# Two transformer layers for one token: attention summed in PSUM quadrants and added to the transposed x, x's rows kept as one PSUM sum, the last softmax ahead of the product before it, 22 arena units kept between the layers

## The chip, the core and the metric

One core of a Trainium2 chip runs the whole program. It has TensorE (matmuls, with a weight load before each), VectorE, ScalarE and GpSimd, SyncE whose queue issues the large transfers here, and 16 DMA engines that bring data from HBM into the on-chip memory (SBUF). Matmuls write to PSUM. The metric is the device time of one execution in microseconds; the time before is 1360.39 us, the median of three runs (1358.34 to 1362.09).

## What is computed

Two batch rows, one new token each, width D = 448. An attention block over a cache of 4096 keys and values (16 heads of 256), then a gated feed-forward block, then both once more with the same weights and the same cache.

```python
def _A_ref(x, k_cache, v_cache, wq, wo):
    q = (x @ wq).reshape(B, Sq, H, Dh).transpose(0, 2, 1, 3)
    scores = jnp.einsum("bhqd,bhkd->bhqk", q, k_cache) * (Dh ** -0.5)
    p = _softmax(scores, axis=-1)
    o = jnp.einsum("bhqk,bhkd->bhqd", p, v_cache)
    return o.transpose(0, 2, 1, 3).reshape(B, Sq, H * Dh) @ wo
def _B_ref(x, W_gate, W_up, W_down):
    gate, up = x @ W_gate, x @ W_up
    return (gate * (gate > 0) * up) @ W_down
x = A_x
x = x + _A_ref(_layernorm(x), A_k_cache, A_v_cache, A_wq, A_wo)
x = x + _B_ref(_layernorm(x), B_W_gate, B_W_up, B_W_down)
x = x + _A_ref(_layernorm(x), A_k_cache, A_v_cache, A_wq, A_wo)
x = x + _B_ref(_layernorm(x), B_W_gate, B_W_up, B_W_down)
```

All data is float32. A pass over the cache is 32 units (head and batch row), each with 4 MiB of keys (k) and 4 MiB of values (v): 256 MiB a pass, twice.

## The kernel before

**Storage.** An arena in SBUF holds 27 slots of 1 MiB: six blocks of four slots and three single slots. A k or v of a unit fills a block or four slots, one quarter each. A head's projection weights (`w_head`: wq and wo of one head) go into a single slot; a `w_in` piece (seven of them, gate and up weights) or `w_out` piece (four, down weights) into any. `pending` is the list of transfers in their order; `pump` issues the next one as soon as a slot is given back by `release`, and SyncE's queue runs them in that order. Which slot a transfer gets is settled when the program is built; on the chip it waits for the last reader of that slot. Eight semaphores take turns, so a transfer also waits until the one issued eight before it has landed. `grouped` decides which k and v are one transfer of 4 MiB and which are four of 1 MiB: the first `SMALL` and the last `ENDS` keys of a pass are cut into quarters.

**Kept units.** The second pass runs over the units in reverse order. What the first pass uses last (the head weights of head 15 and `KEPT` = 20 quarters: k of its last three units and v of its last two) stays in the arena and isn't loaded again. That leaves 6 slots for the feed-forward weights between the passes.

**Order of work.** `attention` is a loop over u with a software pipeline written out by hand. In round u: VectorE scores unit u (32 multiply-and-sum instructions, eight for each quarter, `score`); TensorE, VectorE and ScalarE do the softmax of unit u - 1 in pieces (`softmax_turn`, `softmax_exp`, `softmax_sum`) between the quarters; TensorE multiplies the weights of unit u - 1 with its v (`weigh`, 16 matmuls that trace as 32 records, four column groups of PSUM at a time); ScalarE copies that out (`out_copy`); and unit u - 2 is turned (`out_turn`, `out_keep`) and, for every second unit, projected with wo into `acc` (`project`). Each engine runs its instructions in the order written. Scores of kept units are written to PSUM scratch (`pf`) rather than over the k.

**Between the passes.** `acc` is a PSUM sum that starts with x itself (`seed`). `ffn` takes it, subtracts the mean (`center`: statistics, aggregate and subtraction on VectorE, a turn on TensorE, copies), so that `xr` holds the centred x transposed, 16 times side by side; multiplies with the gate pieces, then with the up pieces (`proj`, four column groups), squares and sums for the deviation, forms the product, turns it, and multiplies with w_out. After the first feed-forward the result is not centred anew: its row sums and its turned rows are added to `xr` (lines 495 to 519), and x's rows are put together again a little later for the next `acc` (`rows`, `keep_rows`, two copies to `x_sb`).

## Time and profile before

| | |
|---|---|
| median of three runs | 1360.39 us |
| the profiled execution | 1357.76 us, span 1355.9 us |
| TensorE, VectorE, ScalarE busy | 54%, 57%, 9% of the span |
| chain that ended last | VectorE 43%, unknown queue 26%, DMA 25%, TensorE 4% |
| HBM read | 563.61 MB, 416 GB/s over the span |
| mean granted TensorE clock | 0.704 |

The page gives busy time by engine, the span in 40 slices, the transfer queues and the costliest groups. Beside it the trace can be asked for stretches of time (busy time of each engine in turn with its instruction count, the granted clock of TensorE, the share in which the 16 DMA engines were busy, GB/s), for the chain of waits, for one engine's timeline (start, length, engine, line, operation, out<-in, count, idle time before and what ended it), and for the transfers of one line with their time from issue to landing.

### The profile page before, as it was taken

The numbers are of one execution on the slowest core, as the hardware profiler recorded it, in microseconds if no ns is written. First come the engines' busy times: TensorE is split into PE (matmuls) and PEld (weight loads), VectorE is DVE, ScalarE is ACT, GpSimd is POOL, SyncE is SP. The second block draws the span as 40 slices with busy tenths as digits, with TensorE's granted clock in tenths as the row PEclk, the third lists the DMA queues.
The fourth block names the chain that finished last, engine by engine and source line by source line (L and its number), as shares of the span: only waits on it lengthen the run. The fifth ranks groups of instructions, "written<-read, shape, count | busy, mean of one in ns | idle before, by whom it ended". The sixth has DMA issues, their size and how long they took to land.

```text
span 1355.9 us, 13276 instructions
## 1 busy us (share of the span) xinstructions
PE 733.1 (54%) x3908; PEld 333.9 (25%) x3908; DVE 778.8 (57%) x4474; ACT 119.5 (9%) x312; POOL 0.7 (0%) x6
## 2 busy tenths in 40 slices
PE   2545546555445553554576674545356464554647
PEld 2322212222122221222232332222122221222212
DVE  6564564645646556456629884554645546556461
ACT  1100000000000000000111110000000000000001
POOL 0000000000000000000000000000000000000000
PEclk7667667775676776767796777676676666776669
DMA  9999999999999999999969999999999999999994
GB/s 402 435 432 428 429 432 429 434 429 427 431 429 430 433 430 427 431 428 434 366 255 404 430 429 431 428 429 431 430 429 432 431 430 429 430 427 434 432 409 184
DMA packets 27585, 564.48 MB, mean 416 GB/s; under 512 B 3060, under 2 KB 3064, under 8 KB 9848
## 3 DMA queue, kind: packets, MB, share of 16 engines
q1 hardware_dynamic: 27508, 563.63, 97.6%
q8 instruction: 31, 0.51, 0.2%
q14 instruction: 42, 0.34, 0.1%
q10 hardware_dynamic: 4, 0.00, 0.0%
HBM read 563.61 MB, written 0.00 MB: 416 GB/s over the span
## 4 chain that ended last, share of the span: by engine, by line
DVE 43%; another core or an unknown queue 26%; DMA 25%; PE 4%; issue 1%; ACT 0%; SPq 0%; DVEq 0%; ACTq 0%
DVE arena L303 38%; DMA arena<-in_k_cache_dram 21%; DVE pf L303 3%; DMA arena<-in_w_in_dram 2%; DMA arena<-in_w_out_dram 2%; PE acc L384 1%; PE po L349 1%; PE pq L250 1%; DVE m L321 1%; DVE ri L339 1%; PE pf L437 0%; DVE mx L312 0%; DVE ri L337 0%; SPq L115 0%
## 5 line engine op out<-in xcount | busy, mean ns | idle before, releaser
L303 DVE SCALAR_TENSOR_TENSOR arena<-arena 128x256 f32<-128x256 f32 x1952 | 686.6, 414 | 489.0 <-DMA arena<-in_k_cache_dram 465.6
L349 PE MATMUL po<-arena,probs 128*2 128x512 f32 x2048 | 304.3, 744 | 58.1 <-DMA arena<-in_v_cache_dram 58.0
L323 PE MATMUL small<-m,ones 1*128 1x1 f32 x128 | 36.3, 351 | 398.2 <-DVE m L321 398.2
L303 DVE DVE_READ_ACCUMULATOR arena<-arena 128x1 f32 x1952 | 149.8, 77 | 0.0
L250 PE MATMUL pq<-arena,xr 128*128 128x256 f32 x384 | 123.1, 467 | 14.4 <-DMA arena<-in_w_head_dram 12.9
L323 PEld LDWEIGHTS small<-m,ones 1*128 1x128 f32 x128 | 30.9, 298 | 403.8 <-DVE m L321 398.0
L349 PEld LDWEIGHTS po<-arena,probs 128*2 128x2 f32 x2048 | 53.8, 97 | 253.2 <-issue 188.5
L384 PE MATMUL acc<-arena,oT 128*2 128x448 f32 x128 | 97.1, 910 | 25.4 <-DVE oT L376 25.4
L250 PEld LDWEIGHTS pq<-arena,xr 128*128 128x128 f32 x384 | 85.8, 240 | 70.8 <-DMA arena<-in_w_head_dram 50.6
L367 PE MATMUL small<-ri,row 128*128 128x1 f32 x512 | 67.4, 253 | 33.3 <-ACT row L360 33.3
L367 PEld LDWEIGHTS small<-ri,row 128*128 128x128 f32 x512 | 61.9, 191 | 47.1 <-ACT row L360 47.1
L360 ACT ACTIVATE row<-po 128x512 f32<-128x512 f32 x64 | 38.2, 597 | 383.6 <-PE po L349 383.6
L333 PE MATMUL small<-rs,ones 128*128 128x1 f32 x128 | 37.3, 360 | 59.6 <-ACT probs L329 59.6
L326 ACT ACTIVATE nm<-small,nsr 128x1 f32<-128x1 f32 x64 | 16.7, 262 | 520.8 <-PE small L323 520.8
L333 PEld LDWEIGHTS small<-rs,ones 128*128 128x128 f32 x128 | 31.8, 309 | 65.0 <-ACT probs L329 65.0
L258 PEld LDWEIGHTS pq<-arena,xr 128*128 128x128 f32 x256 | 44.0, 215 | 4.7
L258 PE MATMUL pq<-arena,xr 128*128 128x128 f32 x256 | 43.7, 299 | 0.0
L275 ACT ACTIVATE arena<-pq 128x512 f32<-128x512 f32 x29 | 17.3, 598 | 273.1 <-PE pq L258 273.1
L303 DVE SCALAR_TENSOR_TENSOR pf<-arena,pq 128x256 f32<-128x256 f32 x64 | 26.2, 442 | 12.8 <-ACT row L360 7.4
L384 PEld LDWEIGHTS acc<-arena,oT 128*2 128x2 f32 x128 | 10.8, 103 | 66.4 <-issue 38.3
L329 ACT ACTIVATE probs<-scores,nm,sr 128x32 f32<-128x32 f32 x64 | 26.4, 413 | 2.1
L316 PE MATMUL small<-ident,mx 128*1 128x128 f32 x64 | 17.4, 272 | 15.4 <-DVE mx L312 15.4
(80 smaller groups left out, 185.5 us busy)
## 6 DMA issues: line engine op xcount, KB each, us to landing
arena<-in_k_cache_dram SPq DMA_DIRECT2D x59, 4096.0 KB, 50.9
arena<-in_v_cache_dram SPq DMA_DIRECT2D x59, 4096.0 KB, 54.8
arena<-in_w_head_dram SPq DMA_DIRECT2D x31, 896.0 KB, 42.1
arena<-in_w_in_dram SPq DMA_DIRECT2D x14, 896.0 KB, 22.7
arena<-in_v_cache_dram SPq DMA_DIRECT2D x12, 1024.0 KB, 38.9
arena<-in_k_cache_dram SPq DMA_DIRECT2D x8, 1024.0 KB, 7.1
arena<-in_w_out_dram SPq DMA_DIRECT2D x4, 896.0 KB, 12.6
arena<-in_w_out_dram SPq DMA_DIRECT2D x4, 672.0 KB, 12.8
```

The costliest lines, as they stand in the source:

```text
L250: nc.tensor.matmul(pq[:, b, :], xT[:, c, b : b + 1].to_broadcast([P, P]), w[:, c * DH : (c + 1) * DH], start=(c == 0), stop=False,)
L258: nc.tensor.matmul(pq[:, b, j * P : (j + 1) * P], xT[:, FULL + j, b : b + 1].to_broadcast([P, P]), w[:, FULL * DH : FULL * DH + P], start= ...
L275: nc.scalar.activation(q, pq, AF.Copy)
L303: nc.vector.scalar_tensor_tensor(prod, kt[:, t, :], 1.0, q_of[u], op0=ALU.mult, op1=ALU.mult, accum_out=s_of[u][:, n : n + 1],)
L316: nc.tensor.transpose(p1, mx_of.pop(u), ident)
L323: nc.tensor.matmul(p2, ones[:1].to_broadcast([1, P]), m1, start=True, stop=True)
L329: nc.scalar.activation(p_of[u], s_of.pop(u), AF.Exp, bias=nm, scale=sr[:, b : b + 1], accum_out=rs)
L333: nc.tensor.matmul(r_of[u], ones.to_broadcast([P, P]), rs, start=True, stop=True)
L349: nc.tensor.matmul(po_of[u][32 * t : 32 * t + 2, :], p_of[u][:, n : n + 2], vt[:, 2 * t * DH : (2 * t + 2) * DH], start=(c == 0), stop=(c ...
L360: nc.scalar.activation(row, po_of.pop(u), AF.Copy)
L367: nc.tensor.matmul(pT_of[u][:, c : c + 1], row[:, at : at + P], r_of[u][:, i : i + 1], start=(i == 0), stop=(i == 1),)
L384: nc.tensor.matmul(acc, oT_of[h][:, c, :], wo[:, c * D : (c + 1) * D], start=False, stop=(u == n_u - 1 and c == 1),)
```

## The change

It does six things. `acc` becomes a whole PSUM tile: the projections of successive units go to three row quadrants (rows 0, 32, 64) instead of two rows. A helper `absorb` replaces `center` and the lines that added the feed-forward result: it copies the given rows to SBUF with their row sums, forms minus the mean by a small matmul, turns the rows by matmuls with `lead` (which also sums the quadrants), and adds both to `xr`. x's rows are one PSUM sum `y` (rows 96 and 97 of the same tile) over the whole program, to which `add_rows` adds with one matmul each time; `x_sb`, `seed`, `rows` and `keep_rows` go. In the last round of a pass, the turn and exponential of the last unit come before the v product of the unit before it. `ENDS` goes from 4 to 12, so the last k and the last two v of a pass come in quarters. And one more v quarter is kept (22 units with the head weights), with the first head transfer of the second pass behind three k quarters.

```diff
-SMALL = 14
-ENDS = 4
+SUMS = 96
+SMALL = 13
+ENDS = 12
...
     keep = {of_second[0], *[key for key in of_second if key[0] != "h"][:KEPT]}
+    keep.add(("v", second[2], NC - 1))
     of_second = [key for key in of_second if key not in keep]
+    of_second.insert(NC - 1, of_second.pop(0))
...
-    x_sb = consts.tile([B, D], F32, name="x_sb")
-    nc.scalar.dma_start(x_sb, x.rearrange("b s d -> (b s) d"))
+    nc.scalar.dma_start(row[:B, :D], x.rearrange("b s d -> (b s) d"))
...
-    acc = ps_a.tile([B, D], F32, name="acc")
-    def seed(y):
-        nc.tensor.matmul(y, ident[:B, :B], x_sb, start=True, stop=False)
+    acc = ps_a.tile([P, D], F32, name="acc")
+    nc.vector.memset(acc, 0.0)
+    y = acc[SUMS : SUMS + B]
...
-    def center(y):
-        st = work.tile([B, 6], F32, name="st")
-        nc.vector.bn_stats(st, y)
-        mv = work.tile([B, 2], F32, name="mv")
-        nc.vector.bn_aggr(mv, st)
-        nc.vector.tensor_scalar_sub(row[:B, :D], y, mv[:, 0:1])
+    def absorb(rows, n, rhs, nrhs):
+        sums = work.tile([P, 1], F32, name="sums")
+        nc.scalar.activation(row[:n, :D], rows, AF.Copy, accum_out=sums[:n])
+        minus = ps_s.tile([P, B], F32, name="small")
+        nc.tensor.matmul(minus, sums[:n].to_broadcast([n, P]), nrhs[:n], start=True, stop=True)
         pt = ps_s.tile([P, DC, B], F32, name="small")
-        turned(pt, row[:B], ident[:B, :B], start=True, stop=True)
-        for p, c in spans:
-            x_c = pt[p, c, None, :]
-            nc.vector.tensor_copy(xr[p, c], x_c.to_broadcast([x_c.shape[0], x_c.shape[1], 16, B]))
+        turned(pt, row[:n], rhs[:n], start=True, stop=True)
+        less = work.tile([P, B], F32, name="less")
+        nc.vector.tensor_copy(less, minus)
+        for part in (less[:, None, :].to_broadcast([P, DC, B]), pt):
+            for p, c in spans:
+                x_c = xr[p, c]
+                nc.vector.tensor_add(x_c, x_c, part[p, c, None, :].to_broadcast(x_c.shape))
+    def add_rows(n, rhs, start=False, stop=False):
+        nc.tensor.matmul(y, rhs[:n], row[:n, :D], start=start, stop=stop)
...
             for c in range(2):
+                n = u - 1 + c
+                at = 32 * (n % 3)
                 nc.tensor.matmul(
-                    acc, oT_of[h][:, c, :], wo[:, c * D : (c + 1) * D],
-                    start=False, stop=(u == n_u - 1 and c == 1),
+                    acc[at : at + B], oT_of[h][:, c, :], wo[:, c * D : (c + 1) * D],
+                    start=(n < 3), stop=(n >= n_u - 3),
                 )
...
-            if_pair(softmax_turn, u - 1)
+            if u < n_u:
+                if_pair(softmax_turn, u - 1)
...
-            if_pair(softmax_exp, u - 1)
+            if u < n_u:
+                if_pair(softmax_exp, u - 1)
...
             if_pair(softmax_max, u)
+            if u == n_u - 1:
+                softmax_turn(u)
+                softmax_exp(u)
             for c in range(NC):
                 if_pair(weigh, u - 1, c)
...
-        center(acc)
-        nc.scalar.activation(x_sb, acc, AF.Copy)
+        absorb(acc[:SUMS], SUMS, lead, nlead)
         total = squares()
...
+        add_rows(SUMS, lead)
         deviation(total)
...
         if last:
-            return rows()
...
+            nc.scalar.activation(row[:, :D], pd, AF.Copy)
+            add_rows(P, scaled, stop=True)
+        else:
+            absorb(pd, P, scaled, nscaled)
+        return scaled
...
-    center(x_sb)
+    absorb(row[:B, :D], B, ident[:, :B], nident)
+    add_rows(B, ident[:, :B], start=True)
     attention(first, keep, lambda: None)
-    rows = ffn(False)
-    attention(second, set(), lambda: keep_rows(rows()))
-    nc.vector.tensor_copy(row[:B, :D], ffn(True))
+    scaled = ffn(False)
+    attention(second, set(), lambda: add_rows(P, scaled))
+    ffn(True)
+    found = row[SUMS : SUMS + B, :D]
+    nc.vector.tensor_copy(found, y)
```

On TensorE, where the first pass ends and the first feed-forward begins. Before (`small` is a small PSUM tile, `po` the v products of a unit, `pf` the feed-forward sums):

```order
L349 MATMUL po<-arena,probs 2x512 x16
L316 MATMUL small<-ident,mx 1x128
L367 MATMUL small<-ri_2836,row 128x1 x4
L323 MATMUL small<-m_2864,ones 128x1
L333 MATMUL small<-rs,ones 128x1
L349 MATMUL po<-arena,probs 2x512 x16
L367 MATMUL small<-ri_2879,row 128x1 x4
L384 MATMUL acc<-arena,oT 2x448 x2
L203 MATMUL small<-ident,row 128x2 x3
L205 MATMUL small<-ident,row 64x2 x2
L437 MATMUL pf<-arena,xr 32x448 x16
```

Now:

```order
L329 MATMUL small<-ident,mx 1x128
L336 MATMUL small<-m_2855,ones 128x1
L346 MATMUL small<-rs,ones 128x1
L362 MATMUL po<-arena,probs 2x512 x16
L380 MATMUL small<-ri_2849,row 128x1 x4
L362 MATMUL po<-arena,probs 2x512 x16
L380 MATMUL small<-ri_2892,row 128x1 x4
L399 MATMUL acc<-arena,oT 2x448 x2
L221 MATMUL small<-nlead,sums 128x2
L209 MATMUL small<-lead,row 128x2 x3
L211 MATMUL small<-lead,row 64x2 x2
L455 MATMUL pf<-arena,xr 32x448 x16
```

The three matmuls of the last softmax (`mx`, `m`, `rs`) stand ahead of both v products; the two products have only the turn of the former between them; and the sum of the mean (`nlead`) is a matmul ahead of the turn of x.

On SyncE's queue, from the last k of the first pass to the first transfers of the second. Before:

```order
L115 DMA arena<-in_k_cache_dram 128x8192
L115 DMA arena<-in_v_cache_dram 128x8192
L115 DMA arena<-in_v_cache_dram 128x2048 x4
L115 DMA arena<-in_w_in_dram 128x1792 x7
L115 DMA arena<-in_w_out_dram 128x1792
L115 DMA arena<-in_w_out_dram 128x1344
L115 DMA arena<-in_w_out_dram 128x1792
L115 DMA arena<-in_w_out_dram 128x1344
L115 DMA arena<-in_w_head_dram 128x1792
L115 DMA arena<-in_k_cache_dram 128x2048 x4
L115 DMA arena<-in_v_cache_dram 128x2048 x4
L115 DMA arena<-in_w_head_dram 128x1792
```

Now:

```order
L117 DMA arena<-in_k_cache_dram 128x2048 x4
L117 DMA arena<-in_v_cache_dram 128x2048 x8
L117 DMA arena<-in_w_in_dram 128x1792 x7
L117 DMA arena<-in_w_out_dram 128x1792
L117 DMA arena<-in_w_out_dram 128x1344
L117 DMA arena<-in_w_out_dram 128x1792
L117 DMA arena<-in_w_out_dram 128x1344
L117 DMA arena<-in_k_cache_dram 128x2048 x3
L117 DMA arena<-in_w_head_dram 128x1792
L117 DMA arena<-in_k_cache_dram 128x2048
L117 DMA arena<-in_v_cache_dram 128x2048 x3
L117 DMA arena<-in_w_head_dram 128x1792
```

The last k and both last v of the first pass come in quarters, the head's weights moved behind three k quarters, and the v that follows has three quarters instead of four.

Of the seven w_in pieces, the sixth now waits for the slot of the first w_in piece, the seventh for that of the second; before, the seventh waited for the first. The first k quarter of the second pass takes the slot of the last w_in piece, the next two those of the first two w_out pieces, and the fourth that of the first kept k quarter to be scored; before, the four took the slots of the four w_out pieces, and the first v quarter that of the first kept k quarter.

More of the change, by code (lines that the diff above doesn't have):

```diff
@@ L176, in two_layers @@
     nc.vector.reduce_sum(lead, ident.rearrange("p (m r) -> p r m", r=32)[:, :2], axis=AX.X)
+    nlead = consts.tile([P, B], F32, name="nlead")
+    nc.vector.tensor_scalar_mul(nlead, lead, -1.0 / D)
     sel = consts.tile([P, B], F32, name="sel")
@@ L396, in attention @@
         begun()
-        seed(acc)
         ahead = 2 if ("k", order[0], 0) in keep else 0
@@ L494, in ffn @@
             release("out", "", j)
-        dn = row[:, :D]
-        sums = work.tile([P, 1], F32, name="sums")
-        nc.scalar.activation(dn, pd, AF.Copy, accum_out=sums)
-        def rows():
-            y = ps_f.tile([P, D], F32, name="pf")[:B]
-            seed(y)
-            nc.tensor.matmul(y, scaled, dn, start=False, stop=True)
-            return y
-        if last:
-            return rows()
-        minus = ps_s.tile([P, B], F32, name="small")
-        nc.tensor.matmul(minus, sums.to_broadcast([P, P]), nscaled, start=True, stop=True)
-        pt = ps_s.tile([P, DC, B], F32, name="small")
-        turned(pt, dn, scaled, start=True, stop=True)
-        less = work.tile([P, B], F32, name="less")
-        nc.vector.tensor_copy(less, minus)
-        for part in (less[:, None, :].to_broadcast([P, DC, B]), pt):
-            for p, c in spans:
-                x_c = xr[p, c]
-                nc.vector.tensor_add(x_c, x_c, part[p, c, None, :].to_broadcast(x_c.shape))
-        return rows
-    def keep_rows(rows):
-        nc.scalar.activation(x_sb, rows, AF.Copy)
-    center(x_sb)
-    attention(first, keep, lambda: None)
-    rows = ffn(False)
-    attention(second, set(), lambda: keep_rows(rows()))
-    nc.vector.tensor_copy(row[:B, :D], ffn(True))
-    nc.sync.dma_start(out.rearrange("b s d -> (b s) d"), row[:B, :D])
+        if last:
+            nc.scalar.activation(row[:, :D], pd, AF.Copy)
[3 more added lines that the diff above has]
+        return scaled
+    nident = work.tile([B, B], F32, name="nident")
+    nc.vector.tensor_scalar_mul(nident, ident[:B, :B], -1.0 / D)
+    absorb(row[:B, :D], B, ident[:, :B], nident)
+    add_rows(B, ident[:, :B], start=True)
+    attention(first, keep, lambda: None)
+    scaled = ffn(False)
[3 more added lines that the diff above has]
+    nc.vector.tensor_copy(found, y)
+    nc.sync.dma_start(out.rearrange("b s d -> (b s) d"), found)
 _OUTS = [((B, 1, D), "float32")]
```

## The prediction

> **What bounds the kernel now.** I read the page first, then the stretches of time around the two feed-forward parts, then the chain of waits, then single transfers and the engines' timelines there.
>
> ```profile
> span 1355.9 us, 13276 instructions
> DMA  9999999999999999999969999999999999999994
> q1 hardware_dynamic: 27508, 563.63, 97.6%
> q8 instruction: 31, 0.51, 0.2%
> 300.00:600.00 300.00, 152.74 (x808) 69.47 (x807) 171.12 (x1000) 23.85 (x64) 0.00 (x0) 0.69 1.00 430
> ```
>
> The transfer queue is busy 97.6% of the span and no compute engine is near that. In the steady stretch it moves 430 GB/s, so a quarter of a k or v block (1,048,576 bytes) costs 2.44 us, a w_in piece (917,504) 2.13, the smaller w_out piece 1.60. Only two places have slack: the slice with the 6, and the end.
>
> ```profile
> 676.00:680.00 4.00, 3.11 (x16) 0.98 (x20) 0.55 (x3) 0.77 (x3) 0.00 (x0) 0.66 0.07 31
> 684.00:688.00 4.00, 2.16 (x9) 0.67 (x8) 1.56 (x4) 0.00 (x0) 0.00 (x0) 1.00 0.06 27
> 1342.00:1344.00 2.00, 2.00 (x24) 0.65 (x20) 0.29 (x2) 0.17 (x1) 0.00 (x0) 1.00 0.06 25
> 694.72 8.46 DMA arena<-in_w_out_dram
> 1333.29 17.16 DMA arena<-in_w_out_dram
> 1350.49 0.95 PE pf L487 x6
> ```
>
> The last two columns of a stretch are the DMA share and GB/s. A share of 0.06 is one engine of sixteen, and 27 GB/s is a sixteenth of 430: one DMA engine is some 12 us behind the fifteen others and works alone. A transfer has landed only when that one has done its part, so the late engine's stream is the clock of this kernel. At the end it governs outright: the last w_out, issued at 1333.29, lands at 1350.45, and TensorE waits for it. Why it is late is not needed here (the instruction queue's 0.51 MB would fit, if it rides on that engine).
>
> In the middle the late engine stops only briefly:
>
> ```profile
> L115 SPq DMA_DIRECT2D arena<-in_w_in_dram x1: 327/327/327, 672.1 to 672.1; - x1
> DMA to landing us min/median/max: 17.8/17.8/17.8
> 690.52 0.33 SPq L115 DMA_DIRECT2D arena<-in_w_in_dram  x1
> DMA to landing us min/median/max: 5.0/5.0/5.0
> ```
>
> The sixth w_in piece lands at 672.1 + 17.8 = 689.9. The seventh waits for an arena slot, which the first feed-forward matmuls free; it is issued at 690.52 and lands 5.0 later, 2.13 of it transfer and 2.9 latency. The four w_out follow without a break, to 694.72 + 8.46 = 703.18. Call that moment T. So the middle costs the late engine about 3.4 us, not the 16 us for which the others idle.
>
> **The change part by part.** *Quarters at the end of a pass, and the last softmax moved up.*
>
> ```profile
> 652.06 0.18 DVE L312 TENSOR_REDUCE mx<-scores 128x1 f32<-128x32 f32 x1
> 656.54 0.43 DVE L303 SCALAR_TENSOR_TENSOR pf<-arena,pq 128x256 f32<-128x256 f32 x1 [4.29 <-DMA arena<-in_k_cache_dram]
> 671.48 0.18 DVE L312 TENSOR_REDUCE mx<-scores 128x1 f32<-128x32 f32 x1
> 674.41 0.28 DVE L321 TENSOR_REDUCE m<-small 1x1 f32<-1x128 f32 x1 [2.75 <-PE small L316]
> 675.89 0.38 PE L323 MATMUL small<-m,ones 1*128 1x1 f32 x2
> 669.98 4.19 PE L349 MATMUL po<-arena,probs 128*2 128x512 f32 x29
> 677.57 5.15 PE L349 MATMUL po<-arena,probs 128*2 128x512 f32 x32
> 1281.21 3.61 PE L349 MATMUL po<-arena,probs 128*2 128x512 f32 x32
> L115 SPq DMA_DIRECT2D arena<-in_v_cache_dram x1: 328/328/328, 636.5 to 636.5; - x1
> DMA to landing us min/median/max: 40.5/40.5/40.5
> 682.80 0.60 ACT L360 ACTIVATE row<-po 128x512 f32<-128x512 f32 x1 [5.70 <-PE po L349]
> 684.75 1.66 PE L384 MATMUL acc<-arena,oT 128*2 128x448 f32 x4 [0.25 <-DVE oT L376]
> 686.45 0.62 DVE L212 BATCH_NORM_STATS2 st<-acc 2x6 f32<-2x448 f32 x1 [1.76 <-PE acc L384]
> 689.50 0.96 PE L437 MATMUL pf<-arena,xr 128*32 128x448 f32 x8 [0.36 <-DVE xr L220]
> ```
>
> The last unit (31) of the first pass has its k in one block, for which VectorE idles 4.29 us until 656.54. In quarters the first lands 3 x 2.44 = 7.3 earlier, at 649.2, so scoring starts when VectorE is free, at 652.24: 4.3 us earlier; each quarter takes about 3.6 to score, so the others are in time. The maximum ends at 667.4 instead of 671.66.
>
> Now the softmax of unit 31 comes before the v product of unit 30 on TensorE, which therefore waits for that maximum. The way from maximum to product is a transpose (0.31 to the reduction at 674.41), the reduction (0.3) and 1.68 (675.89 to 677.57): 2.3 at full clock, 2.7 at half. Product 30 starts at 670.1; before, it ran from 669.98 to 674.17 ahead of softmax 31. From a cold array I give it 5.15, to 675.3. Its copy (0.60) and turn (1.05) take 1.8, as from 682.72 to 684.50, and product 31 starts at 677.1 instead of 677.57, when the last v quarter (636.5 + 40.5 = 677.0) has just landed.
>
> Product 31 at full clock takes 3.61, from cold 5.15. I take full clock, because TensorE has no pause over 0.8 us before it. The Trainium skill, "TensorE: Matmul & The Clock Gate", Part 1, has the clock fall to half after an idle window of about 3.4 us, by which product 31 would stay fast and end at 680.7. The trace does not quite agree: the granted share was 0.66 in 676 to 680, with TensorE busy 3.11 of the 4 us, and by that product 31 could take its 5.15 and end at 682.2. By rows I take 680.7, keep 682.2 for the range, and as its far end 686.3, where both products run at half clock throughout (twice 3.61 each).
>
> Copy, turn and oT take 2.03 (682.72 to 684.75): 682.8. *Quadrants*: the projection's four records now go to two column groups of PSUM. No row shows two groups; four groups do 8 records in 0.96, one group 4 in 1.66. Between 0.5 and 1.66 I take 0.95: 683.7 against 686.41.
>
> *Added to the transposed x.* The mean, the subtraction and the turn took 686.41 to 689.50, 3.1 us. The new helper is what the second pass already starts with:
>
> ```profile
> 704.29 0.54 ACT L498 ACTIVATE row<-pf 128x448 f32<-128x448 f32 x1 [4.97 <-PE pf L487]
> 706.61 1.57 PE L250 MATMUL pq<-arena,xr 128*128 128x256 f32 x6 [0.36 <-DVE xr L518]
> 709.49 0.42 DVE L303 SCALAR_TENSOR_TENSOR arena<-arena 128x256 f32<-128x256 f32 x1 [2.23 <-ACT arena L286]
> ```
>
> 2.32 us, with a row sum, five small matmuls and six additions. The feed-forward starts at 686.05, 3.45 earlier. At the start of the program it replaces the same work under the first k's transfer:
>
> ```profile
> 10.37 0.38 ACT L286 ACTIVATE arena<-pq 128x256 f32<-128x256 f32 x1 [7.78 <-PE pq L258]
> 15.26 0.42 DVE L303 SCALAR_TENSOR_TENSOR arena<-arena 128x256 f32<-128x256 f32 x1 [8.05 <-DMA arena<-in_k_cache_dram]
> ```
>
> The query is there at 10.75 and the transfer at 15.26; only an excess over 4.5 us would show, and the whole helper is 2.32.
>
> *x's rows as one PSUM sum* takes two copies and three seeding matmuls away (off the path) and adds one two-record matmul (0.9) between the gate and up products. In the middle that lies under the wait for w_in, at the end under the wait for w_out; uncovered it would cost 0.9.
>
> *22 units kept.* One quarter less is loaded: -2.44. But five slots are left for w_in, not six, so two pieces follow the first release instead of one. In the new order the sixth w_in is issued at 690.52 - 3.45 = 687.07 and lands at 692.1, the seventh at 694.2, and T = 703.18 - 3.45 + 2.13 = 701.9: 1.3 us earlier. Without the earlier start T would be 2.1 later.
>
> Does the missing quarter then count? After T the slots limit the stream:
>
> ```profile
> 712.37 0.33 SPq L115 DMA_DIRECT2D arena<-in_v_cache_dram  x1
> DMA to landing us min/median/max: 5.4/5.4/5.4
> 723.99 0.33 SPq L115 DMA_DIRECT2D arena<-in_k_cache_dram  x1
> DMA to landing us min/median/max: 7.1/7.1/7.1
> 736.49 0.33 SPq L115 DMA_DIRECT2D arena<-in_v_cache_dram  x1
> ```
>
> The issue at 712.37 waits for the first kept k quarter to be scored, 9.2 after T; the fifth such release is at 723.99. That is 2.9 us a quarter, slower than the stream's 2.44. Before, four k quarters and a head filled the gap and the first v quarter landed without a break. Now the fourth k quarter itself waits for the first score: three quarters and the head end at T + 9.45, and it lands at T + 9.2 + 5.4 = T + 14.6, a pause of 2.7. The kept quarter takes one place out of the row, so the next k again belongs to the fifth release (723.99 - T in both), and the whole v behind it waits for the first product of the pass (736.49). From there on both programs stand alike, relative to T. The 2.44 is given back; what stays is T's 1.3. I keep -2.44 as the other bound. The h14 issue moved behind three quarters lands at T + 9.45, before its queries.
>
> *The end.* The late engine's stream runs on unbroken, so the earlier softmax, quadrants and helper win nothing there; the row sum's 0.19 drops out behind the last w_out: -0.1. Sixteen transfers in quarters instead of four whole ones cost between nothing and an issue of 0.33 each for the twelve more; SP is far ahead, so I take +0.3.
>
> Sum: -1.3 + 0.3 - 0.1 = -1.1 us. The profiled execution took 1357.76 us in all (its span is 1355.9) against a median of 1360.39 for the three runs; I take the difference off the median: 1359.3.
>
> **The rivals.** *The stream closes its gaps* (faster). If both products run at full clock, the slot is free before the fifth w_in has landed (about 687.8) and T is 687.8 + 2 x 2.13 + 7.7 = 699.8, 3.4 earlier; if also the paced stretch is not as stiff as I think, 2.44 more: 1354.6 together. For it: 97.6% busy, so a byte less should be time less. Against it: the releases at 712.37 and 723.99, and a cold array before product 30. Decides: sixth w_in issued before 685.
>
> *The start does not come early* (slower). Place: TensorE's queue, where product 30 now stands behind softmax 31. If both products run at half clock, they end 5.6 later than I take and T is 4.3 later than before: 1364.9. If instead VectorE's 4.29 stays, the first matmul is at 690.3 and T at 706.2, 3.0 later: 1363.6; a projection that does not overlap adds 0.7, and both together go to 1369. Decides: from a first matmul at 687.4 on, keeping the 22nd unit is a loss. For it: the order on TensorE and five slots. The Trainium skill, "Perfetto Trace Analysis", DMA Optimizations, says that splitting helps where the DMA engines are generally idle; they are not here, and by that rule the quarters would win nothing, which is the 1363.6 case. The trace speaks against it, because the 4.29 is a wait for a whole block whose first quarter is there.
>
> *The missing byte counts but nothing else* (T as before): 1360.4 - 2.4 = 1358, within the same verdict as the forecast.
>
> **How the numbers follow.** Forecast and the 1358 case 0.46, the closed gaps 0.30, the late start 0.24. A measurement of this kernel can tell about 0.3%, 4.1 us, from no change. The forecast lies well inside; the closed gaps lie beyond 1356.3 but for a little, and of the late start the half clock and the sums lie beyond 1364.5, the single 4.29 just inside. I put faster 0.29, same 0.50, slower 0.21. The likeliest case alone spans 1357 to 1361; the range takes in the closed gaps and the single late starts: 1354.5 to 1364.5.
>
> **What would show it.** Right: five w_in issued, then the single-engine stretch, the sixth w_in at about 687 and T near 702; scoring of unit 31 beginning near 652; a DMA pause of some 2.7 us before the fourth k quarter, with the next k issued 20.8 after T; the last w_out about 1 us earlier than 1350.45, with TensorE waiting for it. Wrong: the first feed-forward matmul after 688; a second pass whose issues come more than 1 us earlier relative to T; or an end that is not a wait for w_out.

## The result: no change that can be measured

| | before | after |
|---|---|---|
| median of 14 runs each, us | 1362.31 (1357.50 to 1367.74) | 1362.14 (1360.14 to 1363.77) |
| profiled execution, us | 1357.76 | 1361.37 |
| T, landing of the last w_out of the first feed-forward, us | 703.18 | 705.06 |
| last w_out of the second, us | 1350.45 | 1353.97 |

The ratio of after to before is 1.0002, with a 95% interval of 0.9989 to 1.0016. The page of after, and its stretches (PE, PEld, DVE, ACT, POOL busy, granted clock, DMA share, GB/s):

```profile
span 1359.6 us, 13315 instructions
q1 hardware_dynamic: 29092, 562.58, 97.4%
300.00:600.00 300.00, 153.32 (x812) 76.44 (x808) 171.12 (x1000) 23.88 (x64) 0.00 (x0) 0.68 1.00 430
676.00:680.00 4.00, 3.27 (x36) 1.60 (x36) 0.46 (x3) 0.60 (x1) 0.00 (x0) 1.00 0.07 27
684.00:688.00 4.00, 2.85 (x18) 2.27 (x20) 1.28 (x8) 1.91 (x3) 0.00 (x0) 0.63 0.06 23
688.00:692.00 4.00, 4.00 (x24) 0.98 (x20) 0.29 (x2) 0.00 (x0) 0.00 (x0) 0.51 0.41 112
```

The steady stretch is as before. New is the clock column of the last two rows: from about 685 to 691 TensorE ran at half clock. Before, it had 1.00 there, and its gate product took 3.21 us:

```profile
688.00:692.00 4.00, 3.53 (x38) 1.87 (x42) 0.93 (x6) 1.82 (x2) 0.00 (x0) 1.00 0.19 35
689.50 3.21 PE L437 MATMUL pf<-arena,xr 128*32 128x448 f32 x32 [0.36 <-DVE xr L220]
```

VectorE's row of after for the last maximum and TensorE's rows from there to T (start, busy time, then what ended the idle time):

```profile
667.01 0.18 DVE L325 TENSOR_REDUCE mx<-scores 128x1 f32<-128x32 f32 x1
670.07 5.95 PE L362 MATMUL po<-arena,probs 128*2 128x512 f32 x32
677.73 3.62 PE L362 MATMUL po<-arena,probs 128*2 128x512 f32 x32
683.42 0.92 PE L399 MATMUL acc<-arena,oT 128*2 128x448 f32 x4 [0.25 <-DVE oT L389]
685.58 1.42 PE L209 MATMUL small<-lead,row 96*128 96x2 f32 x6
687.67 5.28 PE L455 MATMUL pf<-arena,xr 128*32 128x448 f32 x32 [0.36 <-DVE xr L229]
705.11 0.95 PE L506 MATMUL pf<-arena,row 128*32 128x448 f32 x6 [0.69 <-DMA arena<-in_w_out_dram]
1354.02 0.95 PE L506 MATMUL pf<-arena,row 128*32 128x448 f32 x6 [0.66 <-DMA arena<-in_w_out_dram]
```

The maximum comes 4.47 us earlier than before (its row starts at 667.01 against 671.48). The feed-forward's first matmul comes only 1.83 earlier (687.67 against 689.50) and its gate product takes 5.28 instead of 3.21. The last w_out is waited for until 705.11, where before it was 703.23; in the runs below T is read from this row, less the 0.05 us by which it follows the landing, and where TensorE does not wait for it (old_softmax, before_22, warm_wide_best) from the landing itself. The sixth w_in, and what follows T on SyncE's queue:

```profile
L117 SPq DMA_DIRECT2D arena<-in_w_in_dram x1: 328/328/328, 689.4 to 689.4; - x1
DMA to landing us min/median/max: 4.5/4.5/4.5
715.18 0.33 SPq L117 DMA_DIRECT2D arena<-in_k_cache_dram  x1
726.80 8.93 SPq L117 DMA_DIRECT2D arena<-in_k_cache_dram  x4
738.37 0.33 SPq L117 DMA_DIRECT2D arena<-in_v_cache_dram  x1
```

The sixth piece is issued at 689.4, the fourth k quarter at T+10.1, the fifth release is at T+21.7, and the whole v is issued at T+33.31. Before, the whole v was issued at 736.49, which is also T+33.31.

### The profile page after: what moved, and what is told of

It is laid out like the page before. It is cut to its first block, busy times and chain, and to the rows that moved or that the text cites. A ratio compares the mean times of both kernels' runs of the same rounds, so it can differ in the third digit from the quotient of the medians.

```text
span 1359.6 us, 13315 instructions
## 1 busy us (share of the span) xinstructions
PE 730.1 (54%) x3912; PEld 355.7 (26%) x3912; DVE 777.3 (57%) x4480; ACT 119.7 (9%) x314; POOL 0.7 (0%) x6
## 3 DMA queue, kind: packets, MB, share of 16 engines
q1 hardware_dynamic: 29092, 562.58, 97.4%
## 4 chain that ended last, share of the span: by engine, by line
DVE 38%; DMA 35%; another core or an unknown queue 21%; PE 5%; issue 1%; ACT 0%; SPq 0%; DVEq 0%; ACTq 0%
DVE arena L316 33%; DMA arena<-in_k_cache_dram 20%; DMA arena<-in_w_head_dram 10%; DVE pf L316 3%; DMA arena<-in_v_cache_dram 2%; DMA arena<-in_w_out_dram 2%; DMA arena<-in_w_in_dram 1%; PE po L362 1%; PE pq L263 1%; DVE m L334 1%; PE pf L455 1%; PE acc L399 1%; DVE ri L352 1%; PE pq L271 0%
## 5 line engine op out<-in xcount | busy, mean ns | idle before, releaser
L362 PE MATMUL po<-arena,probs 128*2 128x512 f32 x2048 | 299.7, 737 | 60.5 <-DMA arena<-in_v_cache_dram 60.4
L263 PE MATMUL pq<-arena,xr 128*128 128x256 f32 x384 | 152.9, 558 | 49.8 <-DMA arena<-in_w_head_dram 48.9
L263 PEld LDWEIGHTS pq<-arena,xr 128*128 128x128 f32 x384 | 104.2, 290 | 114.1 <-DMA arena<-in_w_head_dram 87.1
L380 PE MATMUL small<-ri,row 128*128 128x1 f32 x512 | 67.4, 253 | 34.2 <-ACT row L373 34.2
L399 PE MATMUL acc<-arena,oT 128*2 128x448 f32 x128 | 52.1, 913 | 25.5 <-DVE oT L389 25.5
L271 PEld LDWEIGHTS pq<-arena,xr 128*128 128x128 f32 x256 | 52.9, 255 | 7.5
L271 PE MATMUL pq<-arena,xr 128*128 128x128 f32 x256 | 50.7, 334 | 0.0
L389 DVE COPY oT<-small 128x2 f32<-128x2 f32 x64 | 9.2, 144 | 31.6 <-PE small L380 31.6
```

Of the source, the lines that this page charges most:

```text
L263: nc.tensor.matmul(pq[:, b, :], xT[:, c, b : b + 1].to_broadcast([P, P]), w[:, c * DH : (c + 1) * DH], start=(c == 0), stop=False,)
L271: nc.tensor.matmul(pq[:, b, j * P : (j + 1) * P], xT[:, FULL + j, b : b + 1].to_broadcast([P, P]), w[:, FULL * DH : FULL * DH + P], start= ...
L362: nc.tensor.matmul(po_of[u][32 * t : 32 * t + 2, :], p_of[u][:, n : n + 2], vt[:, 2 * t * DH : (2 * t + 2) * DH], start=(c == 0), stop=(c ...
L380: nc.tensor.matmul(pT_of[u][:, c : c + 1], row[:, at : at + P], r_of[u][:, i : i + 1], start=(i == 0), stop=(i == 1),)
L399: nc.tensor.matmul(acc[at : at + B], oT_of[h][:, c, :], wo[:, c * D : (c + 1) * D], start=(n < 3), stop=(n >= n_u - 3),)
```

## The experiments

Twelve kernels, each beside the kernel before on the same chip. "Time" is the profiled execution's own, so that it can be set against the T of the same execution. (The runs were made in four sets; the medians of before in them were 1362.25, 1362.26, 1362.86 and 1363.52, so differences of a microsecond between sets say nothing.)

| run | median | ratio to before, 95% interval | time | T | time - T |
|---|---|---|---|---|---|
| before | 1362.31 | | 1357.76 | 703.18 | 654.6 |
| after | 1362.14 | 1.0002 [0.9989, 1.0016] | 1361.37 | 705.06 | 656.3 |
| k21 | 1358.80 | 0.9986 [0.9971, 1.0001] | 1358.91 | 702.62 | 656.3 |
| old_softmax | 1359.48 | 0.9994 [0.9981, 1.0008] | 1360.84 | 702.13 | 658.7 |
| k21_old_softmax | 1357.14 | 0.9975 [0.9964, 0.9986] | 1356.24 | 700.19 | 656.0 |
| ends4 | 1368.84 | 1.0067 [1.0055, 1.0079] | 1366.54 | 709.78 | 656.8 |
| before_22 | 1365.65 | 1.0029 [1.0014, 1.0045] | 1364.49 | 706.89 | 657.6 |
| k20_old_softmax | 1357.65 | 0.9968 [0.9953, 0.9983] | 1357.46 | 700.52 | 656.9 |
| warm_after | 1363.82 | 1.0016 [1.0000, 1.0031] | 1363.16 | 706.53 | 656.6 |
| warm_k21_old_softmax | 1356.85 | 0.9962 [0.9946, 0.9978] | 1356.82 | 700.21 | 656.6 |
| warm_wide_after | 1358.15 | 0.9967 [0.9950, 0.9983] | 1358.44 | 701.75 | 656.7 |
| warm_wide_best | 1356.12 | 0.9954 [0.9936, 0.9972] | 1355.23 | 700.14 | 655.1 |
| instr12 | 1356.73 | 0.9963 [0.9947, 0.9979] | 1357.01 | 700.96 | 656.0 |
| warm_wide_before | 1357.67 | 0.9960 [0.9945, 0.9975] | 1357.68 | 703.05 | 654.6 |

Over almost ten us of T the last column moves by four, and most of its rows lie between 656 and 657: T carries most of the difference, as the prediction had it. The two kernels without any part of the change (before, warm_wide_before) stand lowest, at 654.6; "The end" below comes back to that.

**The 22nd unit, undone.** In the changed kernel:

```diff
-SMALL = 13
+SMALL = 14
-    keep.add(("v", second[2], NC - 1))
-    of_second.insert(NC - 1, of_second.pop(0))
```

> The changed kernel with 21 units kept instead of 22 and the head's weights first again (six w_in pieces fit before the feed-forward). In the changed kernel's trace the last w_out of the first feed-forward lands at T = 705.06. If the 22nd unit is paid for before T (one more w_in piece behind the first release) and its saved quarter given back after T: T about 702.9, no pause before the fourth k quarter, the rest unchanged relative to T, so 2.1 us faster than the changed kernel. If the quarter's bytes count: T also 2.1 earlier, but 2.4 more between T and the end, so no gain or 0.3 slower.

SyncE's queue of this kernel around T:

```profile
688.97 0.33 SPq L117 DMA_DIRECT2D arena<-in_w_in_dram  x1
735.94 0.33 SPq L117 DMA_DIRECT2D arena<-in_v_cache_dram  x1
```

One w_in piece waits for a slot instead of two, T is 2.44 earlier, and the whole v is issued at T+33.3 although a quarter more is loaded. The time falls by 3.3 us. Keeping one unit more lost time here.

**The last softmax, put back.** The two calls at the end of unit 31 go, and with them the two conditions that skip its softmax in the next round:

```diff
-            if u < n_u:
-                if_pair(softmax_turn, u - 1)
+            if_pair(softmax_turn, u - 1)
...
-            if u == n_u - 1:
-                softmax_turn(u)
-                softmax_exp(u)
```

> The changed kernel with the last softmax back behind the product of unit 30. If the early softmax holds product 30 back behind the maximum of unit 31 (667.2): product 30 runs from about 665.5 as its v lands, product 31 starts near 673.6 and follows its v quarters to about 678.3 instead of 681.35, the feed-forward starts 3.0 earlier, T = 702.0, 3.0 us faster than the changed kernel. If moving it up is a gain: product 31 starts later than 677.73 and T is later by 1 to 2 us.

TensorE of this kernel:

```profile
663.40 1.04 PE L362 MATMUL po<-arena,probs 128*2 128x512 f32 x2
664.21 6.46 PE L362 MATMUL po<-arena,probs 128*2 128x512 f32 x30
673.94 2.76 PE L362 MATMUL po<-arena,probs 128*2 128x512 f32 x24
677.39 1.04 PE L362 MATMUL po<-arena,probs 128*2 128x512 f32 x8 [0.69 <-DMA arena<-in_v_cache_dram]
683.99 6.07 PE L450 MATMUL pf<-arena,xr 128*32 128x448 f32 x32 [0.35 <-DVE xr L229]
```

Product 30 starts at 663.4, among the records of the projection before it, and not behind the last maximum at 670.07. Product 31 is then held only by the last v quarter, and the feed-forward starts at 683.99, 3.7 us before that of the changed kernel. T is 702.13 where 702.0 was expected, and the time falls by 2.7.

**Both undone.**

> Both undone. By the two theories above together: six w_in land by 690.2 without a pause, the seventh is issued near 686.5 and lands at 692.4, T = 700.1, 5 us earlier, and 5 us faster than the changed kernel (1357). If either part of the change is a gain, no faster than the changed kernel.

T is 700.19, the time 1357.14: the two parts add up to within 1 us (3.3 and 2.7 alone, 5.0 together). The late engine works on without a break from 678 to 686 (DMA share 0.05 to 0.11), until the other fifteen get the next piece; this is the rival case in which the stream closes its gaps, reached by undoing two parts of the change.

**Whole blocks again at the end of a pass** (`ENDS = 4` in the changed kernel).

> The changed kernel with the last blocks of a pass whole again, apart from the last v. If VectorE's wait for a whole k sets the start of the last scores: scoring of unit 31 starts at 656.5 instead of 652.1, everything up to T comes 4.3 later, T = 709.4 and 4.3 us slower. If cutting transfers wins nothing while the DMA engines are busy: the same time.

VectorE's wait, and TensorE's rows, of this kernel:

```profile
656.58 0.43 DVE L316 SCALAR_TENSOR_TENSOR pf<-arena,pq 128x256 f32<-128x256 f32 x1 [4.33 <-DMA arena<-in_k_cache_dram]
692.31 5.64 PE L455 MATMUL pf<-arena,xr 128*32 128x448 f32 x32 [0.36 <-DVE xr L229]
709.83 0.95 PE L506 MATMUL pf<-arena,row 128*32 128x448 f32 x6 [0.69 <-DMA arena<-in_w_out_dram]
```

The 4.33 us wait for a whole block is back, the first matmul is 4.64 later and T 4.72 later. Of the three parts that were taken out alone, the quarters are the only one whose loss cost time. The quadrants, the helper and x's rows as one sum were not taken out alone.

**The 22nd unit alone**, in the kernel before (`keep.add(("v", second[2], NC - 1))`, `SMALL = 13`).

> The kernel before with one edit alone: the 22nd unit is kept (the last quarter of the third unit's v), with the head still first. T is the landing of the last w_out of the first feed-forward, 703.18 before. Theory (slots): two w_in pieces wait for the first feed-forward matmuls instead of one, T about 705.3; the missing quarter is given back after T, since the fourth k quarter waits for the first score (issued about T+9.2) and the whole v is issued at T+33.3 as before; time +2.1 us, about 1364.4 beside 1362.3. Rival (bytes count): the quarter that is not loaded is worth 2.44, T +2.1 and 2.4 back: -0.3. Rival (bytes count and the stream closes the wait): -2.4.

SyncE's queue of this kernel, the last w_out's issue and landing, and TensorE's w_out product:

```profile
690.85 1.08 SPq L115 DMA_DIRECT2D arena<-in_w_in_dram  x2
L115 SPq DMA_DIRECT2D arena<-in_w_out_dram x1: 328/328/328, 697.9 to 697.9; - x1
DMA to landing us min/median/max: 9.0/9.0/9.0
703.78 5.54 PE L488 MATMUL pf<-arena,row 128*32 128x448 f32 x28 [0.66 <-DVE row L470]
743.32 0.33 SPq L115 DMA_DIRECT2D arena<-in_v_cache_dram  x1
```

Two w_in pieces wait, and T is 706.89, where I had expected 705.3; about 1 us of the 1.6 is the first of the two, which lands 6.0 after its issue instead of 5.0. I had expected the whole v at T+33.3; it is issued at T+36.4. The w_out product and the query after it ran at half clock in this execution (5.54 us for 28 records, which take 3.2 at full clock), which I had not allowed for; that lies around and behind T. The median is 3.4 us above before, so neither rival holds.

**One unit fewer still** (`KEPT = 19`, `SMALL = 15`, on top of k21_old_softmax).

> The changed kernel with the last softmax back behind the product and 20 units kept instead of 21, so one quarter more is loaded, ahead of the k quarters after T. 21 kept with the same order measured 1357.1. Theory (after T the arena's slots pace the stream, about 3.0 us a quarter against 2.44 of transfer): no w_in waits for a slot, T stays at about 700.0; the extra quarter pushes the first v quarter from 715.2 to about 717.2, and the paced quarters catch up by 0.5 each, so that the whole v is issued at about 734.9 as with 21: 1357.1, no change (0 to +0.5). Rival (bytes count): +2.4, 1359.5. Rival (each unit fewer gains, as from 22 to 21): -2.3, 1354.8.

No w_in waits any more, one quarter more is loaded, and the time is 1357.65 against 1357.14: no change, as the theory of paced slots had it. The 12 runs lie within 1.2 us of each other, 1357.28 to 1358.47; where one piece waits for TensorE (k21_old_softmax) they spread over 3.5, and where two wait (after) over 3.6.

**TensorE kept busy, narrow matmuls.** In the changed kernel a helper issues 128x64 matmuls at each wait from unit 31 to the next query, in both passes, 2 to 8 at a time:

```diff
+    def warm(n, out=None):
+        if n and out is None:
+            out = ps_q.tile([P, B, DH], F32, name="pq")[:, 0]
+        for _ in range(n):
+            nc.tensor.matmul(out[:, :64], ident, ident[:, :64], start=True, stop=True)
```

> The changed kernel with small extra matmuls on TensorE (128x64, into PSUM that is not in use then) wherever it waits from the last scores of a pass to the query of the next. They compute nothing that is used. Theory (half clock cost the predicted 3 us of T): product 30 about 3.6 instead of 5.95, the gate product 3.2 instead of 5.28, product 31 held by the landing of the last v quarter (677.0) and over by 679.1, first feed-forward matmul about 684.9 instead of 687.67, sixth w_in issued about 686 instead of 689.45, T about 702 instead of 705.06, time -3 us against the changed kernel, about 1359.2. Rival (the clock does not matter, the stream or the slots after T decide): T and time as the changed kernel, 1362.1. Rival (the granted clock does not follow how busy TensorE is): product 30 still about 5.9.

Stretches of this kernel, then its rows:

```profile
662.00:666.00 4.00, 4.00 (x17) 2.39 (x16) 3.86 (x20) 0.00 (x0) 0.00 (x0) 0.50 1.01 419
666.00:670.00 4.00, 3.82 (x18) 3.42 (x17) 1.35 (x9) 0.00 (x0) 0.00 (x0) 0.50 0.92 342
670.00:674.00 4.00, 3.81 (x18) 2.53 (x22) 0.14 (x1) 0.77 (x3) 0.00 (x0) 0.50 1.00 358
672.50 5.14 PE L372 MATMUL po<-arena,probs 128*2 128x512 f32 x32
689.21 4.91 PE L470 MATMUL pf<-arena,xr 128*32 128x448 f32 x32
```

A miss: the median is 1363.82, 1.7 above the changed kernel. TensorE is busy 11.6 of 12 us and still has half clock throughout; the extra matmuls, at half clock, also push product 30 back by 2.4 us. This left two readings: the clock does not follow TensorE's work, or it follows something of which these matmuls had little.

**The same on k21_old_softmax**, from the last turn on.

> The best version so far (21 units kept, last softmax behind the product; 1357.1) with the same small extra matmuls from the last turn to the query after T. Theory (T is the stream's there, unbroken at 700.2): the gate product falls from 6.08 to about 3.2 and the seventh w_in is issued 1 us earlier, but T stays at 700.0 to 700.2; the query after T runs at full clock (2.9 to about 1.6 for its first six records), the first score and with it the first v quarter's issue come about 1.1 earlier (710.47 to 709.4), and the whole v at about 733.8: -1.1, 1356.0. Rival (half clock still holds T back): T about 699 and -2 us. Rival (nothing there decides): 1357.1.

T stays, at 700.21, and the median is 0.3 lower where 1.1 was expected: half a miss, inside the spread. The gate product fell only to 4.91. The query after T did run at full clock (1.56 us for its first six records), and the first v quarter was issued at 709.27; but at the end the w_out product ran at half clock (5.89 for 28 records), and this execution ended 8.3 us after the last w_out had landed, where k21_old_softmax took 7.3.

**TensorE kept busy, wide matmuls.** The helper streams 128 to 512 columns in one matmul instead:

```diff
+        nc.tensor.matmul(
+            out[:, : n * P], ident, ident[:, None, :].to_broadcast([P, n, P]),
+            start=True, stop=True,
+        )
```

> The changed kernel with extra matmuls again wherever TensorE waits from the last scores of a pass to the query of the next, but of 128 to 512 columns each instead of 64; they compute nothing that is used. The 64-column ones kept TensorE busy from 661.6 and left the clock at half until 675 all the same. Theory (the clock follows the columns that stream, judged over some 3.4 us at a time): full clock from about 668 on and through the gate product, product 30 about 3.6 to 4.2 instead of 5.95, the gate product 3.2 instead of 5.28, first feed-forward matmul about 685, T about 702 instead of 705.06, time -3 us against the changed kernel's 1362.1. Rival (the clock falls at times of its own whatever TensorE does): a stretch of half clock of 3 us or more still lies between 670 and 690, T 704 to 707, time 1362 to 1364.

This kernel's stretches and rows, the last row from the end of the program:

```profile
662.00:666.00 4.00, 4.00 (x8) 0.95 (x9) 3.83 (x20) 0.00 (x0) 0.00 (x0) 0.54 1.02 423
666.00:670.00 4.00, 2.53 (x8) 0.89 (x7) 1.93 (x10) 0.77 (x3) 0.00 (x0) 0.89 0.96 378
684.00:688.00 4.00, 4.00 (x36) 2.14 (x38) 1.57 (x9) 1.79 (x3) 0.00 (x0) 1.00 0.08 31
670.30 4.70 PE L377 MATMUL po<-arena,probs 128*2 128x512 f32 x32
677.14 3.62 PE L377 MATMUL po<-arena,probs 128*2 128x512 f32 x32
686.18 3.21 PE L479 MATMUL pf<-arena,xr 128*32 128x448 f32 x32
701.80 0.95 PE L530 MATMUL pf<-arena,row 128*32 128x448 f32 x6 [0.66 <-DMA arena<-in_w_out_dram]
1348.86 3.20 PE L530 MATMUL pf<-arena,row 128*32 128x448 f32 x28 [0.66 <-DVE row L512]
```

The gate product is back at 3.21, the feed-forward starts at 686.18, and T is 701.75. The median falls by 4.0 against the changed kernel. In the last row the second feed-forward's w_out product runs through without a wait: TensorE, not the last w_out, now ends this kernel.

**The same on k21_old_softmax.**

> The best version so far (21 units kept, last softmax behind the product, 1357.1) with the same wide extra matmuls from the last turn to the query after T. Theory: full clock through the gate product (3.2 instead of 6.08), T at 700.0 to 700.2 all the same because the stream there is unbroken, the first v quarter after T issued at 709.3 instead of 710.47: 1356.3. With the 64-column ones it was 709.27 and 1356.85. Rival (half clock held T back): T 699, 1355. Rival (the end of the kernel loses what the middle wins): 1357.

1356.12: the fastest version of the study, 6.2 us under the median of before that the result shows, and 6.7 under that of before in its own set. Its 12 runs (1354.71 to 1359.27) overlap with those of k21_old_softmax (1355.25 to 1358.79), so the 1.0 between the two is not told apart from no change.

**A third more instructions for TensorE** (12 tiny matmuls in each of 27 units of both passes, on k21_old_softmax).

> The best version so far (1357.1) with twelve more tiny matmuls (2x1) in each of 27 units of both passes, 648 in all, 2592 records, a third more than TensorE's 7824; they compute nothing that is used. At the 0.51 MB of the first instruction queue that is 0.17 MB more. Theory (this queue rides on the one late transfer engine, at 27 GB/s): that engine gets 3.1 us later in each pass, T about 703.3 instead of 700.2, the last w_out about 6.2 later, 1363.3. Rival (its bytes are spread over sixteen engines): +0.4, 1357.5. Rival (TensorE's own 3 us a unit delay the releases): TensorE or its waits end the chain in the middle of a pass and the DMA share there falls below 1.00.

The instruction queue in this kernel's page, and the wait for the last w_out:

```profile
q8 instruction: 41, 0.67, 0.2%
701.01 0.95 PE L503 MATMUL pf<-arena,row 128*32 128x448 f32 x6 [0.41 <-DMA arena<-in_w_out_dram]
```

The bytes are there, 0.67 MB against 0.51, but T moves by 0.8 and not by 3.1, and the time is 1356.73. The DMA share from 300 to 600 us is 1.00 as without them, so the third case is out too. The suspicion in the prediction that this queue makes one transfer engine late is refuted.

**The kernel before, with wide matmuls.**

> The kernel before, not the changed one, with the same wide extra matmuls (128 to 512 columns, nothing of them is used) wherever TensorE waits from the last scores of a pass to the query of the next. The changed kernel with them measured 1358.15. Before's own times fall into two groups, 1357.4 to 1359.1 and 1360 to 1368, and the profiled one, 1357.76, was of the lower group and had full clock from 680 to 706. Theory (which of the two it is depends on where the half-clock stretches happen to fall between the last product and the query after T): T about 703.2, as in the profile of before, time about 1358 to 1359.3, no upper group; the changed kernel is then worth 0 to -1.1 us at equal clock, as predicted. Rival (the two groups have another cause): the median stays at 1362 and both groups stay.

TensorE of this kernel:

```profile
689.87 3.21 PE L463 MATMUL pf<-arena,xr 128*32 128x448 f32 x32
703.10 0.95 PE L513 MATMUL pf<-arena,row 128*32 128x448 f32 x6 [0.69 <-DMA arena<-in_w_out_dram]
```

The median is 1357.67 and all 12 runs lie between 1356.60 and 1359.55; the plain kernel in the same set went from 1358.10 to 1368.36, with 12 of its 16 runs above 1362. The upper group is gone and T is where the profile of before had it. This fits half clock as the cause of the upper group, but no execution of that group was traced, and the extra matmuls stand at the end of both passes: which stretch of half clock costs, and in which pass, is not shown.

## Why the prediction was right, and where a term was off

**The clock of the kernel** (right). The late engine's stream, read at T, decided most of it: T moved from 700 to 710 and the time with it, but for up to four us between T and the end.

**Quarters** (right). The maximum ends at 667.2 (667.4 predicted), and ends4 gives the 4.3 us back. The Trainium skill, "Perfetto Trace Analysis", DMA Optimizations, names engines that are generally idle as the case in which splitting transfers may help; read as the only case, it would have had the quarters win nothing. This case does not agree: with the queue 97.4% busy they win 4.7 us of T and 6.7 us of the median.

**Softmax ahead of product 30** (start right, sizes off). Product 30 starts at 670.07 (670.1) and takes 5.95 (5.15); product 31 runs at full clock in 3.62 as I took it, and starts 0.6 late. What I did not ask is whether the move was worth its price: product 30 could have run from 663.4, and old_softmax shows that the old place starts the feed-forward 3.7 us earlier in the same surroundings.

**Quadrants** (right): 0.92 us, 0.95 predicted.

**The helper and the way to the sixth w_in: the term that was mis-sized.** I took 2.32 us for the helper and, in "690.52 - 3.45 = 687.07", carried over the pace of before's gate product, both at full clock. In the profile of after the clock fell at about 685: the turn of x took 1.42, the first matmul came at 687.67 instead of 686.05, the first piece was released 1.8 us after it instead of 1.0, and the second another 1.5 later (0.75 in warm_wide_after). The sixth w_in was issued at 689.4, and T was 705.06 instead of 701.9: +1.9 against before, not -1.3. With the clock held up there, these steps land on the forecast: first matmul 686.18, sixth w_in in the row below, T 701.75. SyncE's queue of warm_wide_after:

```profile
687.20 1.08 SPq L117 DMA_DIRECT2D arena<-in_w_in_dram  x2
734.95 0.33 SPq L117 DMA_DIRECT2D arena<-in_v_cache_dram  x1
```

Against warm_wide_before, the kernel before under the same clock, T is 1.30 earlier (701.75 against 703.05). I had forecast 1.3.

**22 units** (right). T pays 2.44 (after against k21) and 1.94 (old_softmax against k21_old_softmax) for 2.13 predicted. The quarter that is not loaded is given back: the whole v is issued 33.2 to 33.3 us after T in before, after, k21, ends4, k20_old_softmax and warm_wide_after alike, with 20, 21 or 22 units kept (34.2 and 34.7 in old_softmax and k21_old_softmax, 34.9 in warm_after, 36.4 in before_22). The rival in which the bytes count is refuted three times.

**The end** (half right). TensorE waits there for the last w_out, as predicted. But from T to the end the profiled execution of after took 656.3 us where before took 654.6, and I had allowed 0.2 for it. The difference is in the stream: the last w_out lands at T+648.9 against T+647.3. Some 1.1 us of it is there already at the head weights that land at T+110.8 before and at T+111.9 after. Ahead of them the query after T ran at half clock (2.50 us for six records that take 1.56 in warm_wide_after), and the first kept quarter was given back at T+10.1 instead of the 9.2 of before. In warm_wide_after these are T+8.9, and T+110.3 for the head weights. But in k21, with T+9.35, the same head weights land at T+112.1, so the query's clock is not the whole of it, and that stays open. The rest is the quarters at the end of the second pass: from the last head weights to the last w_out before, warm_wide_before and ends4 take 73.4 us, after and warm_wide_after 74.0 and 73.8 (I had given 0.3 for this).

In warm_wide_after the last w_out lands at T+647.2, as in before, but the end comes 9.4 us after it instead of 7.3. TensorE's gate product of the second feed-forward and a stretch around it, in warm_wide_after and then in warm_wide_before:

```profile
1326.00:1340.00 14.00, 14.00 (x60) 7.14 (x56) 1.73 (x10) 2.51 (x4) 0.00 (x0) 0.50 0.76 280
1336.63 5.63 PE L479 MATMUL pf<-arena,xr 128*32 128x448 f32 x32
1326.00:1340.00 14.00, 13.68 (x91) 6.12 (x94) 3.05 (x12) 3.18 (x6) 0.00 (x0) 1.00 0.83 316
1338.64 3.21 PE L463 MATMUL pf<-arena,xr 128*32 128x448 f32 x32
```

Counted from T the product starts 0.7 us earlier (T+634.9 against T+635.6), but it runs at half clock and takes 5.63 instead of 3.21, and the matmul behind it that adds to x's rows (0.92) is not covered by a wait: the 0.9 that the prediction named for that case. So T's 1.3 earns no time here. The medians, 1358.15 and 1357.67, come from two sets in which before differed by 0.7, and can't be told apart.

**The sum.** I set it against a median of three runs and took the profiled execution for a typical one. It was of the lower group, with full clock from 680 to 706. The half clock thus took about 3 us from the T that I forecast for after, and, by the medians of before without and with wide matmuls, some 4.6 us from before, so that both medians came out near 1362. That they came out so close is luck as far as the forecast goes: in the one pair of profiled executions T moved the other way, +1.9 where I had -1.3, and nothing in the prediction had before lose time to the clock as well.

**The signs named beforehand.** As forecast, the scoring of unit 31 began at 652.09, the DMA engines paused ahead of the fourth k quarter (share 0.09 from 713.5 to 716, where I had 2.7 us of pause), and the program ended with a wait for the last w_out. The sixth w_in (689.4), T (705.06), the next k (T+21.7, not 20.8) and the last w_out (1353.97, not 1 us earlier than 1350.45) did not come as forecast. The first matmul, at 687.67, stayed short of the 688 that was to show the prediction wrong, but was past the 687.4 from which on the 22nd unit was to be a loss, and it was one.

The rival "the start does not come early" had the right mechanism, half clock, but on products 30 and 31 and at 1364.9; the one that closes the gaps came true only where the new softmax order and the 22nd unit were both taken out.

## What to carry to other kernels

Where one stream sets the pace, find the landing after which everything is paced alike, here T, and judge each edit by what it does to that landing: a stall that ends before it is worth its full size, bytes saved behind it were worth nothing. A unit that is kept on chip takes a slot from the prefetch; count which load then has to wait for a release. And ask of a single profile whether the clock in its critical stretch was luck: the times of the kernel before fell into groups some 4 us apart, and a few wide matmuls in TensorE's waits took the slower ones away. They are no cure for every stretch: at the end of warm_wide_after the clock was at half in spite of them.

## What the runs showed of the hardware

**Busy time alone does not bring the clock up.** In warm_after 64-column matmuls kept TensorE busy 11.6 of 12 us at 0.50 granted. With 128 to 512 columns in each (warm_wide_after) the clock rose at about 666, was at half again from about 669 to 673, stayed at 1.00 from 674 to 696 and fell once more from about 697 to 700. Width alone does not settle it either: from 1326 to 1340 the same execution had TensorE busy 14.0 of 14 us, wide matmuls among them, at 0.50, while warm_wide_before had 1.00 over the same stretch. The Trainium skill, "TensorE: Matmul & The Clock Gate", Part 1, has full clock come after some 3.4 us of sustained activity; by the profile's busy time the stretches at 662 and at 1326 do not agree with it, and what counts as activity stays open. Its remark that the window runs free, so that one kernel differs from run to run, fits the two groups of before; here that was worth 4.6 us (1362.31 against 1357.67).

**One transfer engine falls behind at a steady rate.** From the completions of the sixteen engines on single transfers of k21_old_softmax: the last is 2.1 us after the first at 79 us, 8.0 at 310, 16.6 at 659, then 1.1 at 724 once all have idled, and 15.2 at 1298. That is 2.5% of the time. With a third more TensorE instructions it is 2.2, 8.1, 16.9, 1.0 and 16.2, so they are not its cause; the cause is open. At the end of k21_old_softmax it leaves fifteen engines idle for some 13 us (DMA share 0.03 to 0.28 from 1336 until the last w_out lands at 1348.9), more than any edit of this study moved the time.
